# Attention and two mixture layers on one core: other planner durations and weights for ScalarE, a longer lag for the banks of h

## The chip, the cores and the metric

The kernel runs on one core of one Trainium2 chip. The time is device microseconds of one launch, the median of the runs shown. Engines are named PE (TensorE, matmuls; PEld is its weight load), DVE (VectorE), ACT (ScalarE), POOL (GpSimd) and SP (SyncE, which starts the DMAs). TensorE's granted clock is given as a share of full speed.

## The reference, cut to what matters

```python
def sm_attn(qq, kk, vv):                      # 8 batches, 8 heads of 64, 576 positions
    s = qq @ kk.transpose(0, 1, 3, 2) / 8
    a = np.exp(s - s.max(-1, keepdims=True))
    return (a / (a.sum(-1, keepdims=True) + 1e-9)) @ vv
p_packed = sm_attn(p, k, v)                   # 32 packed queries
x = sm_attn(q, p_packed, p_packed)            # -> 4608 tokens x 512
h = x @ w_in                                  # 512 -> 2048
g = h * np.tanh(np.log1p(np.exp(h)))
x2 = g @ w_out                                # 2048 -> 512
# experts: top one of 8 by x2 @ w_gate, weighted by its softmax probability
out = prob * (np.maximum(x2 @ w1[e], 0) @ w2[e])
```

## The kernel before

A batch has two halves of 288 tokens, 16 halves in all. Every float32 product is made of three matmuls on rounded parts (high times high, high times low, low times high). The attention's second step is folded into the first mixture's weights: `w_in` times the packed keys (`fold`, L457, eight matmuls of each of two PSUM tiles) gives `wp`, and the softmax of the scores (L510 and the DVE and ACT steps behind it, L517 to L553) is multiplied with it.

From about 66 us to 800 us the first mixture runs. Its pieces are, for each half and each 128 columns of h:

- the *product* (L595): six matmuls of 128 x 288 into a bank of `h`, a ring of two PSUM banks,
- `tanh` on ACT (L612), then the copy `hs` of the same bank (by the helper `copy_ways`, L244 on ACT or L245 on DVE). The copy's end frees the bank,
- after eight products, a *group*: the table of ACT is changed (L629), Arctan (L635) and Sin (L637) for four pairs of products, then on DVE the multiplication with hs (L640); `g1`, the rounded copy, by `copy_ways` on POOL, DVE or ACT; `g2`, the remainder, on DVE (L256),
- the *back* product (L608): three matmuls for each of four banks of `acc`.

At the next group's first tanh ACT loads the tanh table again (L612 ACT_TABLE_LOAD). In every batch PE also has the packed scores (L288), transposes (L313, L314), values (L321), and a transpose (L334) of the packed result `pd`; these share the ring `o` of two PSUM banks. Their softmax runs on DVE (maximum L298, L299) and ACT (exponential L302, with a table of its own). `at` and `ae` are the copies of the transposed softmax, `pk` the copy of the packed keys that the fold needs. Up to about 150 us the engines beside PE also convert the words of `w_in` and `w_out` (L398 to L434, `a`, `sgn`, `wi`, `woh`, `wol`).

From about 760 us on the experts run: L874 (h_p), ACT's relu L881, DVE's remainder L886, L894 (y), DVE's L900, with 8 pieces of an expert's weights loaded, rounded (`exh`, `copy_ways`) and subtracted (`exl`, `tensor_ways`) for every expert.

Nothing of this order is written by hand. Every piece is a step of a `Plan` (lines 34 to 165), which emits all steps in the order of a simulated clock in ns: it knows each step's cost on each engine that can do it, a `LATENCY` for each engine, rings with their buffers, and due times. Three things of it are touched here. `SLACK` is added to the end of the step that frees a ring's buffer before the buffer counts as free. `end` (line 106) estimates for a step with several engines when each would finish it; the cost there is multiplied by the engine's `WEIGHT`, and the engine with the earliest estimate takes it. The costs of steps on ACT stand at the calls, and for PSUM copies in `copy_ways`: 51 + 0.833 n on ACT, 69 + 1.03 n on DVE. The weights, costs and lag shape the order only; on the chip each engine takes its instructions in that order and waits for what they need.

Of the kernel before, what the change touches and what calls it, by code (L numbers as in the profile page):

```python
# [15 lines left out]
AF = mybir.ActivationFunctionType  # L16
# [26 lines left out]
             ls=1, x2=8, gm=2, os=2)  # L43


class Plan:
# [5 lines left out]
    LATENCY = dict(PE=70, DVE=128, ACT=190, Pool=117, SP=0, host=0)  # L52
    DMA_LATENCY, DMA_ISSUE, DMA_RATE, DMA_AHEAD = 1900, 450, 360.0, 937
    DMA_SLACK = 1000
    SLACK = dict(h=600)
    SLOWED = dict(DVE=0.3, Pool=0.5)
    WINDOW = 3413
    WEIGHT = dict(DVE=2.41, ACT=1.34, Pool=1.31)

    def __init__(self, rings):  # L60
        self.rings, self.steps = rings, []
# [12 lines left out]
    def run(self):  # L74
# [24 lines left out]
        for _ in range(len(self.steps)):  # L99
# [5 lines left out]

            def end(s, at, e):
                ahead = floor.get(e, now) + sum(cost for key, cost in alone.get(e, ()) if key < s["key"])
                return max(at, ahead) + s["ways"][e][0] * self.WEIGHT[e] + self.LATENCY[e]

            for e in able:  # L110
                mine = None
# [54 lines left out]
def packed_attention_moe_kernel(ctx, tc, pT, kT, v_main, v_tail, qT, w_in, w_out, wg, w1, w2, out):  # L166
# [66 lines left out]
    def step(engine, cost, emit, **kw):  # L233
        return plan.step([(engine, cost, emit)], **kw)

    def copy_ways(dst, src, n, psum=False):

        def on(run):
            def emit():
                d = dst()  # L240
                run(d, src())
            return emit

        ways = [("ACT", (51 if psum else 93) + 0.833 * n, on(lambda d, x: S.activation(out=d, in_=x, func=AF.Copy))),  # L244
                ("DVE", 69 + (1.03 if psum else 0.52) * n, on(lambda d, x: V.tensor_copy(out=d, in_=x)))]  # L245
        if not psum:
            ways.append(("Pool", 160 + 0.835 * n, on(lambda d, x: G.tensor_scalar(  # L247
                out=d, in0=x, scalar1=1.0, scalar2=1.0, op0=ALU.mult, op1=ALU.mult))))
        return ways
# [324 lines left out]
    def moe1(gr, due):  # L574
# [36 lines left out]
        def tanh(n, k):  # L611
            S.activation(out=part(n, "z", k), in_=tiles[n]["p", k], func=AF.Tanh, scale=0.5)  # L612

        for n in pairs:
            c = n % 16 // 4
            z1[n], hc[n] = [], []
            for k in range(2):
                at_k = due + (n + k - n0) * TI
                ins.append(step("PE", 798, lambda n=n, k=k: product(n, k),
                                  after=wp_done[b, c] + a2_done[i, g] + ins[-1:],  # L620
                                  takes=[("h", n + k)], frees=[("wa", ("w", b, c))] * (hf == 1 and (n + k) % 4 == 3)
                                  + [("hl", (i, g * parts))] * ((n + k) % 16 == 15 or parts and (n + k) % 8 == 7), due=at_k))
                z1[n].append(step("ACT", 291, lambda n=n, k=k: tanh(n, k), after=[ins[-1], *z1[n]] + sins.get(gr - 1, []),
                                  takes=[("z", n)] * (k == 0), due=at_k))
                hc[n].append(plan.step(copy_ways(lambda n=n, k=k: part(n, "hs", k), lambda n=n, k=k: tiles[n]["p", k], TK, True),
                                       after=[z1[n][k], *hc[n]], takes=[("hs", n)] * (k == 0), frees=[("h", n + k)], due=at_k))
                b_steps.extend([z1[n][k], hc[n][k]])
# [40 lines left out]
        def evac(d, engine):  # L668
            if d == 0 and not more:
                x2_load(i)  # L670
            if engine == "ACT":
                S.activation(out=x2f[i][:, d], in_=accs[i, d], func=AF.Copy)
            elif more:
                V.tensor_tensor(out=x2f[i][:, d], in0=x2f[i][:, d], in1=accs[i, d], op=ALU.add)
            else:
                V.tensor_copy(out=x2f[i][:, d], in_=accs[i, d])

        for d in range(4):
            ev.append(plan.step([(e, cost, lambda d=d, e=e: evac(d, e)) for e, cost in (("ACT", 291), ("DVE", 365))[more:]],
                                after=[outs[n + 1, d]] + ev[:1], takes=[("x2f", key)] * (d == 0 and not more),  # L680
                                frees=[("acc", (i, d, g * parts))], due=due))
        x2_done[key] = ev
# [43 lines left out]
    def gate_copy(i):  # L726
        l_s = tile_of("ls", [128, TK])
        S.activation(out=l_s, in_=gst[i], func=AF.Copy)
        gst[i] = l_s
# [78 lines left out]
    def gate(i, key, ld, due, exp_after=(), exp_before=None):  # L808
        b, hf = halves[i]
        mm = step("PE", 850, lambda: gate_mm(i), after=[ld, wg_done], takes=[("o", ("l", i))], frees=[("x2f", key)], due=due,  # L810
                  share=0.8)
        cp = step("ACT", 291, lambda: gate_copy(i), after=[mm], takes=[("ls", i)], frees=[("o", ("l", i))], due=due)
        tu = step("PE", 400, lambda: gate_turn(i), after=[cp], takes=[("o", ("t", i))], frees=[("ls", i)], due=due)
        mx = step("DVE", 600, lambda: gate_max(i), after=[tu], frees=[("o", ("t", i))], due=due)
        ex = step("ACT", 113, lambda: gate_exp(i), after=[mx, *exp_after], due=due)
# [63 lines left out]
    def moe2_hi(xk, f, early=False):  # L879
        h = tile_of("g", [128, 2, 2, TK], F32R)[:, :, 0] if early else tile_of("g2", [128, 2, TK], F32R)  # L880
        S.activation(out=h[:, 0], in_=hc[xk, f], func=AF.Relu)  # L881
        hc[xk, f] = hc[xk, f], h
# [25 lines left out]
    def moe2(n, due):  # L908
# [7 lines left out]
                       frees=[("wa", ("e", b, c, x)) for x in "hl"] * (hf == 1 and o == 3)  # L916
                       + x2_at(ring, ("x2", i)) * (f == 7), due=due)
        g = ("g" if early else "g2", ("y", n))
        hi = step("ACT", 291, lambda: moe2_hi(i, f, early), after=[y_in[n], last_g1 if early else open_c], takes=[g], due=due)
        lo = step("DVE", 369, lambda: moe2_lo(i, f), after=[hi], frees=[("h", ("y", n))], due=due)  # L920
        last, ahead[n] = i == NH - 1 and f > 5, (lo, g)
        for d, m in [(d, m) for d in range(4) for m in ((n - 1, n) if last else (n,))] * (not last or f == 7):
# [212 lines left out]
```

## Time and profile before

| | |
|---|---|
| median of 3 runs | 1211.97 us (1211.04 to 1212.27) |
| profiled execution | 1210.29 us |
| its span | 1208.5 us |
| mean granted clock | 0.993 |
| PE busy | 1161.8 us (96%) |
| DVE busy | 676.0 us (56%) |
| ACT busy | 651.1 us (54%) |
| POOL busy | 224.5 us (19%) |

The span is the time between the first and the last record of the profiled execution. An engine's busy time leaves out register, branch, semaphore and DMA-issuing instructions. A wait is the idle time of an engine ahead of an instruction, with the instruction that ended it: "PE h L595 <- ACT hs L244" is PE idle ahead of a matmul of line 595 into h until ACT's copy of line 244.

### The profile page before, as it was taken

What the parts mean: (1) busy time and instruction counts of PE and PEld (TensorE: products, weight loads), DVE (VectorE), ACT (ScalarE), POOL (GpSimd) and SP (SyncE); (2) the same over time, 40 slices, a digit from 0 to 9 for tenths busy, and PEclk for the clock granted to TensorE, in tenths of its full rate; (3) what the DMA queues carried; (4) which work ended last, traced back from release to release, by engine and by line L of the source; (5) the groups of instructions that cost most, each with busy time, mean ns of one, the idle gap of its engine ahead of it and who ended that gap; (6) DMA issues with size and microseconds to landing.
All of it is one profiled execution on the core that took longest, in us unless ns stands there. A gap on an engine that the chain in (4) does not pass through costs nothing.

```text
span 1208.5 us, 23614 instructions
## 1 busy us (share of the span) xinstructions
PE 1161.8 (96%) x9680; PEld 1075.2 (89%) x9681; DVE 676.0 (56%) x1237; ACT 651.1 (54%) x1335; POOL 224.5 (19%) x214
## 2 busy tenths in 40 slices
PE   4699999999999999999999999999999999999998
PEld 1478898898898898898898899999999999999998
DVE  4999955564455454454454464466556473737442
ACT  3687787777777777777777778212122121212110
POOL 2344411011011021021021022112213030302110
PEclk9889999999999999999999999999999999999999
DMA  8856533421331321321321141133425151524411
GB/s 294 307 193 223 206 138 125 175 110 56 153 129 56 134 110 56 133 110 56 133 110 56 55 145 55 50 130 139 152 77 189 58 189 62 189 86 143 146 45 41
DMA packets 37642, 151.48 MB, mean 125 GB/s; under 512 B 4888, under 2 KB 5528, under 8 KB 33944
## 3 DMA queue, kind: packets, MB, share of 16 engines
q1 hardware_dynamic: 37528, 149.90, 34.1%
q8 instruction: 78, 1.28, 0.4%
q14 instruction: 36, 0.29, 0.1%
HBM read 122.04 MB, written 27.84 MB: 124 GB/s over the span
## 4 chain that ended last, share of the span: by engine, by line
PE 76%; DVE 10%; ACT 8%; issue 2%; DMA 2%; POOL 1%; SPq 0%; DVEq 0%; ACTq 0%; POOLq 0%
PE x2p L608 25%; PE y L894 15%; PE h_p L874 15%; PE h L595 14%; PE w_ps L457 2%; DVE z L640 2%; DVE g L256 1%; ACT L612 1%; DMA eraw<-w 1%; ACT z L635 1%; PE o L321 1%; ACT L629 1%; ACT z L612 1%; PE o L510 1%; ACT hs L244 1%
## 5 line engine op out<-in xcount | busy, mean ns | idle before, releaser
L608 PE MATMUL x2p<-g,woh 128*128 128x288 f32 x2048 | 416.6, 297 | 0.0
L608 PEld LDWEIGHTS x2p<-g,woh 128*128 128x128 f32 x2048 | 327.4, 188 | 14.4 <-issue 13.6
L608 PE MATMUL x2p<-g,wol 128*128 128x288 f32 x1024 | 301.9, 295 | 0.0
L595 PEld LDWEIGHTS h<-hl,wp 128*128 128x128 f32 x1536 | 215.2, 191 | 47.0 <-ACT hs L244 35.6
L595 PE MATMUL h<-hl,wp 128*128 128x288 f32 x1536 | 242.1, 303 | 12.6 <-ACT hs L244 12.6
L894 PE MATMUL y<-g,exh 128*128 128x288 f32 x1024 | 211.2, 298 | 1.2 <-DVE os L900 0.5
L881 ACT ACTIVATE g<-h_p 128x288 fp32r<-128x288 f32 x128 | 52.4, 410 | 279.7 <-PE h_p L874 257.4
L608 PEld LDWEIGHTS x2p<-g,wol 128*128 128x128 f32 x1024 | 192.2, 188 | 0.0
L640 DVE TENSOR_TENSOR z<-z,hs 128x576 f32<-128x576 f32 x128 | 95.3, 780 | 147.1 <-ACT z L637 147.1
L894 PEld LDWEIGHTS y<-g,exh 128*128 128x128 f32 x1024 | 162.6, 188 | 9.0 <-issue 4.3
L612 ACT ACTIVATE z<-h 128x288 f32<-128x288 f32 x256 | 105.7, 413 | 108.9 <-PE h L595 102.9
L247 POOL TENSOR_SCALAR g<-z 128x576 fp32r<-128x576 f32 x85 | 78.7, 927 | 454.0 <-DVE z L640 364.9
L874 PE MATMUL h_p<-x2h,exh 128*128 128x288 f32 x512 | 152.0, 297 | 0.0
L874 PE MATMUL h_p<-x2l,exh 128*128 128x288 f32 x512 | 151.0, 295 | 0.0
L874 PE MATMUL h_p<-x2h,exl 128*128 128x288 f32 x512 | 150.7, 294 | 0.0
L894 PE MATMUL y<-g,exl 128*128 128x288 f32 x512 | 150.4, 294 | 0.0
L886 DVE SCALAR_TENSOR_TENSOR g<-h_p,g 128x288 fp32r<-128x288 f32 x128 | 57.7, 451 | 138.4 <-ACT g L881 138.4
L244 ACT ACTIVATE hs<-h 128x288 f32<-128x288 f32 x256 | 104.7, 411 | 0.9 <-DVE z L640 0.9
L256 DVE TENSOR_TENSOR g<-z,g 128x576 fp32r<-128x576 f32 x128 | 94.6, 762 | 15.3 <-POOL g L247 15.2
L874 PEld LDWEIGHTS h_p<-x2h,exh 128*128 128x128 f32 x512 | 96.0, 187 | 0.9 <-DVE x2h L702 0.5
L894 PEld LDWEIGHTS y<-g,exl 128*128 128x128 f32 x512 | 96.5, 189 | 0.0
L874 PEld LDWEIGHTS h_p<-x2l,exh 128*128 128x128 f32 x512 | 96.5, 188 | 0.0
(127 smaller groups left out, 1334.5 us busy)
## 6 DMA issues: line engine op xcount, KB each, us to landing
eraw<-w SPq DMA_DIRECT2D x64, 512.0 KB, 6.2
wi<-wi_d SPq DMA_DIRECT2D x24, 1024.0 KB, 6.7
x2f<-x_d SPq DMA_DIRECT2D x22, 576.0 KB, 4.3
x_d<-x2f SPq DMA_DIRECT2D x20, 576.0 KB, 2.8
raw<-kT SPq DMA_DIRECT2D x16, 576.0 KB, 7.5
q<-qT SPq DMA_DIRECT2D x16, 576.0 KB, 5.3
out<-os SPq DMA_DIRECT2D x15, 576.0 KB
raw<-v_main SPq DMA_DIRECT2D x16, 512.0 KB, 8.5
```

Source lines behind the costliest of these rows:

```text
L244: ways = [("ACT", (51 if psum else 93) + 0.833 * n, on(lambda d, x: S.activation(out=d, in_=x, func=AF.Copy))), ("DVE", 69 + (1.03 if psum ...
L247: ways.append(("Pool", 160 + 0.835 * n, on(lambda d, x: G.tensor_scalar(out=d, in0=x, scalar1=1.0, scalar2=1.0, op0=ALU.mult, op1=ALU.mult))))
L256: engine.tensor_tensor(out=d, in0=a(), in1=b(), op=op)
L457: T.matmul(out=t[i][quarter(x)], lhsT=pk[own[i], b, x], rhs=w_i[c][own[i], x], start=True, stop=True)
L595: T.matmul(out=h, lhsT=wp_t[b, c][:, xw, kt, 128 * o:128 * o + 128], rhs=a2[i, g][:, xa, kt], start=(m == 0), stop=(m == 5))
L608: T.matmul(out=accs[i, d], lhsT=w_o[c][xw][:, o, 128 * d:128 * d + 128], rhs=tiles[n]["g"][:, xg, k], start=(m == 0 and (f == 0 or f == 8 ...
L612: S.activation(out=part(n, "z", k), in_=tiles[n]["p", k], func=AF.Tanh, scale=0.5)
L640: g0 = step("DVE", 669, lambda n=n, z=z: V.tensor_tensor(out=z(), in0=z(), in1=tiles[n]["hs"], op=ALU.mult), after=[si, *hc[n]], frees=[(" ...
L874: T.matmul(out=h_p, lhsT=ex_t[ek, c][xw][:, k, 128 * o:128 * o + 128], rhs=x2s[xk][xx][:, k], start=(n == 0), stop=(n == 11))
L881: S.activation(out=h[:, 0], in_=hc[xk, f], func=AF.Relu)
L886: V.scalar_tensor_tensor(out=h[:, 1], in0=h_p, scalar=0.0, in1=r32(h[:, 0]), op0=ALU.max, op1=ALU.subtract)
L894: T.matmul(out=accs[xk, d], lhsT=ex_t[ek, 2 + c][xw][:, o, 128 * d:128 * d + 128], rhs=hc[xk, f][:, xh], start=(f == 0 and n == 0), stop=( ...
```

## The change

`SLACK` of h goes from 600 to 1000 ns. `WEIGHT` becomes a pair: the first as before, the second when the planner's clock is past `EARLY`, 150 us. In the second DVE's factor is 1.3 (2.41 before), ACT's 1.9 (1.34 before), POOL's the same. Single reads of PSUM by ACT get a cost 16 ns higher: 67 instead of 51 in `copy_ways`, 307 instead of 291 for the tanh, the copy of the result x2f, the gate's copy and the experts' relu. Lines behind line 55 move on by two, so L595 is L597 in the changed kernel, L244 and L245 are L246 and L247, L302 is L304.

```diff
-    SLACK = dict(h=600)
+    SLACK = dict(h=1000)
     SLOWED = dict(DVE=0.3, Pool=0.5)
     WINDOW = 3413
-    WEIGHT = dict(DVE=2.41, ACT=1.34, Pool=1.31)
+
+    EARLY = 150000
+    WEIGHT = dict(DVE=2.41, ACT=1.34, Pool=1.31), dict(DVE=1.3, ACT=1.9, Pool=1.31)
...
-                return max(at, ahead) + s["ways"][e][0] * self.WEIGHT[e] + self.LATENCY[e]
+                return max(at, ahead) + s["ways"][e][0] * self.WEIGHT[now > self.EARLY][e] + self.LATENCY[e]
...
-        ways = [("ACT", (51 if psum else 93) + 0.833 * n, on(lambda d, x: S.activation(out=d, in_=x, func=AF.Copy))),
+        ways = [("ACT", (67 if psum else 93) + 0.833 * n, on(lambda d, x: S.activation(out=d, in_=x, func=AF.Copy))),
...
-                z1[n].append(step("ACT", 291, lambda n=n, k=k: tanh(n, k), after=[ins[-1], *z1[n]] + sins.get(gr - 1, []),
+                z1[n].append(step("ACT", 307, lambda n=n, k=k: tanh(n, k), after=[ins[-1], *z1[n]] + sins.get(gr - 1, []),
...
-        hi = step("ACT", 291, lambda: moe2_hi(i, f, early), after=[y_in[n], last_g1 if early else open_c], takes=[g], due=due)
+        hi = step("ACT", 307, lambda: moe2_hi(i, f, early), after=[y_in[n], last_g1 if early else open_c], takes=[g], due=due)
```

How many instructions of a kind each engine has, counted over the whole order:

| copies | before | after |
|---|---|---|
| hs, h out of its bank | ACT 256 | ACT 128, DVE 128 |
| wp, rounded | ACT 64 | ACT 39, DVE 25 |
| at | ACT 16 | ACT 5, DVE 11 |
| ae | DVE 16 | DVE 5, ACT 11 |
| g1 | ACT 15, DVE 28, POOL 85 | ACT 5, DVE 40, POOL 83 |
| exh | ACT 22, DVE 7, POOL 35 | DVE 16, POOL 48 |
| exl | DVE 57, POOL 7 | DVE 64 |
| x2l (a part of x2) | DVE 16, POOL 16 | DVE 32 |

On PE, nearly every stretch between two pairs of products holds 12 matmuls of the back product where 9 stood, for the same work in all. At a group that follows the packed transposes (L334), in a middle batch, PE's order also turns round. L595 (L597) is the product, L510 (L512) the scores, L457 (L459) the fold, L608 (L610) the back product. Before:

```order
L608 MATMUL x2p_5264<-g,woh 128x288 x2
L608 MATMUL x2p_5264<-g,wol 128x288
L595 MATMUL h<-hl,wp 128x288 x6
L510 MATMUL o<-q,pk 32x288 x8
L595 MATMUL h<-hl,wp 128x288 x12
L457 MATMUL w_ps<-wi,pk 32x512 x8
L595 MATMUL h<-hl,wp 128x288 x12
```

After:

```order
L610 MATMUL x2p_5243<-g,wol 128x288
L512 MATMUL o<-q,pk 32x288 x8
L597 MATMUL h<-hl,wp 128x288 x12
L610 MATMUL x2p_5774<-g,woh 128x288 x2
L610 MATMUL x2p_5774<-g,wol 128x288
L459 MATMUL w_ps<-wi,pk 32x512 x8
L597 MATMUL h<-hl,wp 128x288 x12
```

The scores now stand ahead of the group's first product instead of behind it, and three matmuls of a back product stand ahead of the fold.

On DVE, in the same batch, where the packed softmax's maximum (`sm`) stands among the steps of a group. L640 (L642) is the multiplication with hs, L245 (L247) a copy, L256 (L258) the remainder. Before:

```order
L640 TENSOR_TENSOR z_5291<-z_5291,hs_5293 128x576
L640 TENSOR_TENSOR z_5320<-z_5320,hs_5322 128x576
L256 TENSOR_TENSOR g_5425<-z_5291,g_5425 128x576
L298 TENSOR_REDUCE sm_5442<-ex_5387 128x1
L299 TENSOR_SCALAR sm_5442<-sm_5442 128x1
L298 TENSOR_REDUCE sm_5457<-ex_5399 128x1
L299 TENSOR_SCALAR sm_5457<-sm_5457 128x1
L307 TENSOR_SCALAR sm_5442<-sm_5442 128x1
L308 RECIPROCAL sm_5442<-sm_5442 128x1
L256 TENSOR_TENSOR g_5455<-z_5320,g_5455 128x576
```

After:

```order
L642 TENSOR_TENSOR z_5297<-z_5297,hs_5299 128x576
L300 TENSOR_REDUCE sm_5432<-ex_5378 128x1
L301 TENSOR_SCALAR sm_5432<-sm_5432 128x1
L300 TENSOR_REDUCE sm_5447<-ex_5395 128x1
L301 TENSOR_SCALAR sm_5447<-sm_5447 128x1
L258 TENSOR_TENSOR g_5438<-z_5297,g_5438 128x576
L309 TENSOR_SCALAR sm_5432<-sm_5432 128x1
L310 RECIPROCAL sm_5432<-sm_5432 128x1
L309 TENSOR_SCALAR sm_5447<-sm_5447 128x1
L310 RECIPROCAL sm_5447<-sm_5447 128x1
L642 TENSOR_TENSOR z_5329<-z_5329,hs_5331 128x576
```

Both maxima now come ahead of the third pair's remainder and of the fourth pair's multiplication. Behind that pair's rounding copy and remainder, this queue goes on with copies of h for the next group.

On ACT, at the end of the prelude (about 62 to 66 us before). L329 (L331) is `pd`, the packed result; L612 (L614) the tanh. Before:

```order
L329 ACTIVATE pd_684<-o_712,sm_597 128x64
L637 ACTIVATE z_566<-z_566,b_pi_171 128x576
L637 ACTIVATE z_604<-z_604,b_pi_171 128x576
L244 ACTIVATE pk_168<-o_740 128x128
L612 ACT_TABLE_LOAD
L612 ACTIVATE z_750<-h_638 128x288
L244 ACTIVATE hs_765<-h_638 128x288
```

After:

```order
L246 ACTIVATE g_697<-z_449 128x576
L246 ACTIVATE at_705<-o_690 128x512
L639 ACTIVATE z_562<-z_562,b_pi_171 128x576
L637 ACTIVATE z_608<-z_608,b_half_169 128x576
L639 ACTIVATE z_608<-z_608,b_pi_171 128x576
L331 ACTIVATE pd_684<-o_710,sm_594 128x64
L614 ACT_TABLE_LOAD
L614 ACTIVATE z_743<-h_636 128x288
L246 ACTIVATE hs_747<-h_636 128x288
L614 ACTIVATE z_743<-h_648 128x288
L246 ACTIVATE hs_747<-h_648 128x288
L246 ACTIVATE pk_168<-o_751 128x128
```

The table load and two pairs of tanh and copy now stand ahead of `pk`, and a rounding copy of g ahead of `at`.

## Rows read from the trace of the kernel before

**Rows 1.** Busy time by stretch: each engine's us (count), then clock, DMA share.

```profile
62.00:66.00 4.00, 2.53 (x18) 0.50 (x18) 3.97 (x6) 3.97 (x9) 2.80 (x3) 0.50 0.86 279
66.00:150.00 84.00, 79.56 (x624) 71.22 (x625) 79.94 (x111) 67.00 (x138) 39.33 (x41) 0.98 0.57 201
150.00:800.00 650.00, 641.21 (x5608) 591.97 (x5607) 329.08 (x566) 469.69 (x956) 91.26 (x96) 1.00 0.27 102
800.00:1209.00 409.00, 401.92 (x3066) 391.27 (x3064) 218.95 (x463) 77.61 (x165) 74.76 (x47) 1.00 0.34 119
```

**Rows 2.** PE's waits from 66, 150 and 800 us: total, times, longest.

```profile
PE h L595 <- ACT hs L244: 3.8, 3, 1.6
...
PE h L595 <- ACT hs L244: 8.8, 17, 1.1
...
PE y L894 <- DVE os L900: 0.5, 2, 0.2
PE y L894 <- ACT g L881: 0.5, 1, 0.5
```

**Rows 3.** Chain of waits, one run of back products: start, us.

```profile
690.18 9.54 PE x2p L608 x72
```

**Rows 4.** Timeline at a group's start: start us, us, engine, instruction, [idle before].

```profile
499.50 0.29 PE L608 MATMUL x2p<-g,wol 128*128 128x288 f32 x1
...
500.07 1.87 PE L595 MATMUL h<-hl,wp 128*128 128x288 f32 x12 [0.27 <-ACT hs L244]
```

**Rows 5.** Timeline at the packed softmax's exponential.

```profile
538.49 0.76 DVE L256 TENSOR_TENSOR g<-z,g 128x576 fp32r<-128x576 f32 x1 [0.57 <-POOL g L247]
...
539.16 0.74 DVE L298 TENSOR_REDUCE sm<-ex 128x1 f32<-128x576 f32 x1
...
540.17 1.28 ACT L302 ACT_TABLE_LOAD   x1 [2.45 <-DVE sm L299]
...
542.39 0.29 PE L608 MATMUL x2p<-g,wol 128*128 128x288 f32 x1
...
543.29 0.40 ACT L244 ACTIVATE hs<-h 128x288 f32<-128x288 f32 x1
...
543.74 0.66 PE L595 MATMUL h<-hl,wp 128*128 128x288 f32 x3 [1.06 <-ACT hs L244]
```

**Rows 6.** Timeline at two groups that begin around the scores.

```profile
293.34 0.93 PE L595 MATMUL h<-hl,wp 128*128 128x288 f32 x5 [0.69 <-ACT hs L244]
...
564.05 1.28 ACT L612 ACT_TABLE_LOAD   x1 [0.42 <-PE h L595]
...
566.11 0.92 PE L595 MATMUL h<-hl,wp 128*128 128x288 f32 x5 [0.51 <-ACT hs L244]
...
567.10 1.09 PE L457 MATMUL w_ps<-wi,pk 64*32 64x512 f32 x16
```

**Rows 7.** Timeline at the longest wait between 66 and 150 us.

```profile
139.87 0.66 ACT L400 ACTIVATE a<-word 128x512 f32<-128x512 f32 x1
...
140.87 0.80 PE L595 MATMUL h<-hl,wp 128*128 128x288 f32 x4 [1.62 <-ACT hs L244]
```

**Rows 8.** The page's groups: reads of 288 columns from PSUM, mean ns.

```profile
L886 DVE SCALAR_TENSOR_TENSOR g<-h_p,g 128x288 fp32r<-128x288 f32 x128 | 57.7, 451 | 138.4 <-ACT g L881 138.4
L244 ACT ACTIVATE hs<-h 128x288 f32<-128x288 f32 x256 | 104.7, 411 | 0.9 <-DVE z L640 0.9
```

**Rows 9.** Timeline at the end of the prelude.

```profile
63.58 0.26 ACT L244 ACTIVATE pk<-o 128x128 f32<-128x128 f32 x1
...
63.89 1.96 PE L457 MATMUL w_ps<-wi,pk 64*32 64x512 f32 x16 [1.02 <-ACT pk L244]
```

**Rows 10.** Timeline at the load of an expert's weights.

```profile
925.31 0.41 ACT L881 ACTIVATE g<-h_p 128x288 fp32r<-128x288 f32 x1 [2.78 <-PE h_p L874]
...
928.95 0.45 DVE L886 SCALAR_TENSOR_TENSOR g<-h_p,g 128x288 fp32r<-128x288 f32 x1
929.60 2.74 DVE L245 CAST exh<-eraw 128x1024 fp32r<-128x1024 f32 x1 [0.20 <-DMA eraw<-w]
```

More of the change, by code (lines that the diff above doesn't have):

```diff
@@ L678, in moe1 @@
         for d in range(4):
-            ev.append(plan.step([(e, cost, lambda d=d, e=e: evac(d, e)) for e, cost in (("ACT", 291), ("DVE", 365))[more:]],
+            ev.append(plan.step([(e, cost, lambda d=d, e=e: evac(d, e)) for e, cost in (("ACT", 307), ("DVE", 365))[more:]],
                                 after=[outs[n + 1, d]] + ev[:1], takes=[("x2f", key)] * (d == 0 and not more),
@@ L811, in gate @@
                   share=0.8)
-        cp = step("ACT", 291, lambda: gate_copy(i), after=[mm], takes=[("ls", i)], frees=[("o", ("l", i))], due=due)
+        cp = step("ACT", 307, lambda: gate_copy(i), after=[mm], takes=[("ls", i)], frees=[("o", ("l", i))], due=due)
         tu = step("PE", 400, lambda: gate_turn(i), after=[cp], takes=[("o", ("t", i))], frees=[("ls", i)], due=due)
```

## The prediction

> **What bounds the kernel now.** I read the busy time by stretch first [rows 1]. From 66 us on TensorE (PE) is busy 80 of 84, 641 of 650 and 402 of 409 us: the change takes no matmul away, so all it can give back is idle time of PE, and all the harm it can do is new idle time. The waits come next [rows 2]. Up to 800 us nearly everything that PE waits for is a bank of `h`: the copy of h out of PSUM (`hs`, on ScalarE, ACT) is the last reader of a bank, and there are two banks. That is 3.8 us in 3 waits from 66 to 150 us, and 8.8 us in 17 waits up to 800 us. The experts' stage, behind that, has no such copy, and waits of 1.0 us in all. So the gain is bounded by 12.6 us and by what each restart costs beside its wait. At a group's start the last back product's matmul (L608) begins at 499.50 and the product (L595) at 500.07 [rows 4]; the pace is 0.133 us for a matmul, 9.54 us for 72 [rows 3], so the loss is 0.57 - 0.13 = 0.44 us, where the wait says 0.27. With 0.16 more for each of 20 waits the bound is 12.6 + 3.2 = **15.8 us**.
>
> The waits from 150 us on have three forms.
> *Exponential*, four times 1.06 [rows 5]: VectorE (DVE) takes the softmax's maximum only from 539.16, behind a subtraction (L256) that had itself waited 0.57 us for GpSimd (POOL). ACT loads the table from 540.17, and with two exponentials and a tanh in between, the copy that frees the bank starts at 543.29. PE began its last back product's matmul before that at 542.39.
> *Scores*, three times 0.51 and once 0.69 [rows 6]: the tanh table is loaded at a group's first product (564.05), and PE has only eight score matmuls and one more product to do until the first bank is back.
> *Group start*, seven waits of about 0.3 [rows 4]: table load, tanh and copy against two products and nine matmuls of the back product. Two waits that are left are under 0.15.
>
> **The change part by part.** No work is added or removed. What moves is the engine of a copy, how long the planner keeps PE from a bank, and the place of some matmuls.
>
> 1. *The longer lag (SLACK of h from 600 to 1000 ns) and ACT's durations, 16 ns longer.* A bank comes free later in the plan, so the plan puts more back products between two pairs of products: 12 matmuls in the order where 9 stood, in nearly every pair. Three more are 3 x 0.133 = 0.40 us of cover for each wait. By themselves they cost nothing: the longer runs of back products that follow have three or six less.
>
> Group starts: loss 0.44, cover 0.40, so 7 x 0.40 = **-2.8** (bounds 0 and -3.1).
> Scores: the order has the eight score matmuls first, then two products in one piece, three back matmuls and a fold of 1.09 us [rows 6], then the next bank. The first product ends 0.8 us into the piece; table load 1.28, tanh and copy 0.41 each [rows 6, 8] free its bank at 2.9, or 3.0 with what lies between instructions; PE has 1.6 + 0.4 + 1.1 = 3.1 us of work until then. The wait goes: 3 x (0.51 + 0.16) + 0.69 + 0.16 = 2.9, of which I take **-2.7**. If only the three back matmuls count, it is 4 x 0.40 = -1.6.
>
> 2. *The exponential.* The order of DVE now puts both maxima ahead of the subtraction that had waited, and ahead of the last multiplication. That takes 0.57 us of waiting and two instructions of about 0.76 [rows 5] out of the way: the table load comes up to 2.1 us sooner, at 538.1. From table load to copy were 543.29 - 540.17 = 3.1 us; the same three instructions stand there now (two exponentials, then tanh), so the bank is free at about 538.1 + 3.1 + 0.4 + 0.1 = 541.7. PE, with its three more back matmuls, asks for it at 542.5 + 0.4 = 542.9. What hides the maxima is the work of POOL and ACT ahead of them: if the third multiplication is late, the table is late with it, one for one. For that I leave 0.45 of each loss of 1.06 + 0.16 = 1.22 standing: 4 x 0.77 = **-3.1** (bounds 0 and -4.9).
>
> 3. *66 to 150 us.* The weights don't change there (EARLY is 150 us), only lag and durations do. In the longest wait, 1.62, the copy was late because a conversion (`a`, 0.66) stood ahead of it on ACT [rows 7]. Loss in this stretch: 3.8 + 3 x 0.16 = 4.3. The order has 12 or 15 back matmuls where 6 or 9 stood. I take two thirds, **-2.8** (bounds 0 and -4.3): DVE is busy 80 of 84 us there [rows 1], so a wait can move rather than end.
>
> 4. *Weights after 150 us.* DVE is cheap in the plan now and ACT dear; half of the copies of h, 128 of 256, go to DVE. One costs 0.41 on ACT and 0.45 on DVE, by its nearest row, another read of 288 columns from PSUM [rows 8]. That is 0.04 us more until the bank is back, but ACT can begin the next bank's tanh 0.3 us sooner, so I cost it at nothing; its cover is the 12 back matmuls. Queued behind it on DVE are the multiplications and subtractions that feed the back product; DVE was busy 329 of 650 us [rows 1] and gets 128 x 0.45 = 58 us more. The packed softmax's copies out of PSUM (`at`) go to DVE too and share the two banks of `o`: a new wait in each of six batches, between 0 and 0.5 us (a wait of rows 6), of which I take 0.2: **+1.2** (bounds 0 and +3).
>
> The Trainium skill speaks against this part: VectorE: DVE Perf Modes, section Specifications, has VectorE closer to SBUF and ScalarE closer to PSUM. The rows agree, 0.45 against 0.41 [rows 8]; if PE waited for the difference at each of the 128 copies, it would be 128 x 0.04 = 5 us, and the sum -2.5 in place of -7.5.
>
> 5. *The prelude, up to 66 us.* Here too the order differs through lag and durations. Before, ACT copied `pk` at 63.58, ahead of its tanh table; PE's fold started at 63.89 after a wait of 1.02 [rows 9]. In the new order ACT has a rounding copy of g ahead of `at` (576 columns; from 0.26 us for 128 and 0.41 for 288 I estimate 0.7) and one more `pd`, less one conversion that leaves: some 0.5 to 1.2 us. And the table load and two tanh with two copies stand ahead of `pk`: 1.28 + 4 x 0.3 = 2.5. The fold comes up to 3.7 us later; nine back matmuls are done meanwhile, 1.2 us at pace. Net **+2.5** (bounds 0, if something else holds the fold anyway, and +3.7). The granted clock is 0.50 in this stretch [rows 1], the lower of the two levels; more idle time may keep it there longer, which the range takes in.
>
> 6. *Experts.* ACT gives up its 22 rounding copies of weights; DVE takes nine and POOL 13 of them, and DVE takes POOL's seven subtractions. PE's order is nearly the same. DVE's L886 started 3.2 us after the end of the ACT step it follows (925.72 to 928.95) and PE didn't wait [rows 2, 10]. So **0**, between -1 (all waits of that stage) and the price of the slower rival.
>
> Sum: -2.8 - 2.7 - 3.1 - 2.8 + 1.2 + 2.5 = -7.7, of which I keep **-7.5**. The profiled execution, 1210.29, goes to 1202.8; the median of the runs shown, 1.7 us above it, goes from 1211.97 to **1204.5**.
>
> **The rivals.**
> *All of the waits go.* All 15.8 are covered, the prelude and the `o` banks still cost: -15.8 + 2.5 + 1.2 = -12.1, so 1200. For it: 12 back matmuls in every pair, and half of the copies off ACT. Against it: table load, tanh and copy are as long as before.
> *The gain is swallowed.* The plan's order isn't the chip's time: the exponential's chain stays late (nothing of 3.1), the early waits move (nothing of 2.8), the prelude loses 3.7: -7.7 + 3.1 + 2.8 + 1.2 = -0.6, so 1211.4; with two of the three 1208.5 to 1210.2. For it: tanh stands behind both exponentials now. This is also the case in which the change doesn't do what it says.
> *Slower: DVE is late for the experts.* It has 16 rounding copies where seven stood, two in each load of an expert. At 2.74 us [rows 10] the nine are 25 us more of DVE, in front of L886; a delay of L886 beyond the 3.2 us is on PE's path. With half of the 25 there it is 1204.5 + 12.5 = 1217. It decides when two such copies stand between an L881 and its L886. Against it: seven of them ran with waits of 1.0 us in all [rows 2], and POOL's subtraction, which ran beside one, is gone.
>
> By the Trainium skill (SBUF — State Buffer, Who interferes with whom) a DVE copy in a two-port mode and a GpSimd instruction lock each other out of a shared port pair for a whole instruction. If each of the nine casts met a rounding copy on POOL so, the time would be this rival's 1217. No row here shows PE waiting for it.
>
> **How the numbers follow.** Forecast 0.55 (1202 to 1208), all of the waits 0.14 (1198 to 1202), swallowed 0.18 (1208.5 to 1212.5), slower 0.13 (from 1214.5). The range takes the first, part of the second and the third: 1199.5 to 1212.5. A measurement of this kernel can tell about 0.2%, 2.4 us, from no change. Faster by more: 0.55 + 0.14 + a little of the third, 0.71; within it: 0.16; slower by more: 0.13.
>
> **What the changed profile would show.** Waits of L595 for hs from 150 to 800 us under 3 us, in place of 8.8; the exponential's table load about 2 us sooner against the products beside it; the fold in the prelude at about 66 to 67.5; PE busy as before from 800 us on. I am wrong if PE waits for DVE's copy of h in many groups, if the clock stays at 0.50 beyond 70 us, or if L894 waits for L886 at the loads of experts.

## The result and the profile after

The changed kernel takes 1200.13 us in the median of four runs (1199.23 to 1201.89), the kernel before 1211.51 beside it: a ratio of 0.9912, with a 95% interval from 0.9897 to 0.9928. The time lies in the range of the prediction, 4.4 us below its 1204.5. The profiled execution took 1200.09 us with a span of 1198.3, which is 10.2 us less than before (1210.29 and 1208.5).

Busy time of the changed kernel by stretch, in the columns of [rows 1]:

```profile
62.00:66.00 4.00, 3.19 (x18) 2.34 (x15) 2.83 (x5) 3.94 (x8) 2.60 (x4) 0.50 0.58 170
66.00:150.00 84.00, 80.28 (x637) 69.56 (x638) 78.79 (x111) 62.77 (x130) 40.86 (x45) 0.96 0.60 209
150.00:800.00 650.00, 648.85 (x5682) 602.41 (x5681) 432.88 (x814) 399.64 (x758) 81.81 (x84) 1.00 0.28 104
800.00:1198.00 398.00, 390.81 (x2986) 381.63 (x2984) 218.72 (x463) 55.36 (x140) 62.89 (x42) 1.00 0.33 119
```

From 150 to 800 us PE is now busy 648.9 of 650 us, where it was 641.2. DVE has 104 us more to do there and ACT 70 less. PE's waits of the changed kernel from 66, 150 and 800 us, to be set beside [rows 2]:

```profile
PE h L597 <- ACT hs L246: 1.6, 3, 0.8
PE w_ps L459 <- ACT pk L246: 0.9, 1, 0.9
PE x2p L610 <- ACT x2f L674: 0.9, 1, 0.9
PE x2p L610 <- DVE g L258: 0.7, 1, 0.7
...
PE h L597 <- ACT hs L246: 0.9, 4, 0.2
PE x2p L610 <- DVE g L258: 0.2, 1, 0.2
...
PE h_p L876 <- DVE g L888: 1.8, 3, 0.8
```

The 17 waits of the middle stretch, 8.8 us, are four of 0.9 us. They are the four exponentials; the group starts and the scores have none left. From 66 to 150 us the waits for h fell from 3.8 to 1.6 us, but two of 0.9 and 0.7 us for the back product's banks (x2p) came, and one of 0.9 at the fold.

*Exponential.* Timeline of the changed kernel at the place of [rows 5]:

```profile
532.38 0.75 DVE L642 TENSOR_TENSOR z<-z,hs 128x576 f32<-128x576 f32 x1
533.04 0.74 DVE L300 TENSOR_REDUCE sm<-ex 128x1 f32<-128x576 f32 x1
...
534.05 1.28 ACT L304 ACT_TABLE_LOAD   x1 [0.96 <-DVE sm L301]
534.05 1.76 PE L597 MATMUL h<-hl,wp 128*128 128x288 f32 x12
...
537.10 0.29 PE L610 MATMUL x2p<-g,wol 128*128 128x288 f32 x1
537.17 0.39 ACT L246 ACTIVATE hs<-h 128x288 f32<-128x288 f32 x1
...
537.62 1.06 PE L597 MATMUL h<-hl,wp 128*128 128x288 f32 x6 [0.23 <-ACT hs L246]
```

The table load begins with the products beside it, no longer 0.8 us behind them, and its copy starts 3.12 us later, as it did (543.29 - 540.17). Of the wait of 1.06 us, 0.23 is left. The 0.83 between them is the table load's alone, since PE has 12 back matmuls between these two pairs of products in both kernels. Matmuls into x2p (busy, count, clock) before and after:

```profile
539.60:543.60 4.00, 1.74 (x12) 1.00 0.00 0
534.30:537.50 3.20, 1.74 (x12) 1.00 0.00 0
```

*Scores.* Timeline at the place of [rows 6]:

```profile
556.31 1.28 ACT L614 ACT_TABLE_LOAD   x1
...
557.62 1.85 PE L597 MATMUL h<-hl,wp 128*128 128x288 f32 x12
...
558.71 0.41 ACT L614 ACTIVATE z<-h 128x288 f32<-128x288 f32 x1 [1.11 <-PE h L597]
559.34 0.42 DVE L247 COPY hs<-h 128x288 f32<-128x288 f32 x1
...
559.80 1.09 PE L459 MATMUL w_ps<-wi,pk 64*32 64x512 f32 x16
```

ACT has loaded the table 1.3 us ahead of the group's first product and then waits for PE. Before, it came to the load with four copies of x2f behind it, and only when the product was done.

*Group start.* Timeline at the place of [rows 4]:

```profile
493.10 1.28 ACT L614 ACT_TABLE_LOAD   x1 [0.39 <-PE h L597]
...
494.70 0.41 ACT L246 ACTIVATE hs<-h 128x288 f32<-128x288 f32 x1
...
495.11 0.29 PE L610 MATMUL x2p<-g,wol 128*128 128x288 f32 x1
495.24 1.79 PE L597 MATMUL h<-hl,wp 128*128 128x288 f32 x12
```

The last back matmul and the product stand 0.13 us apart, PE's pace. The copy's end at 495.11 falls together with the end of the twelve matmuls: three more of them were just enough.

*Prelude.* Timeline of the changed kernel at the place of [rows 9]:

```profile
63.60 1.28 ACT L614 ACT_TABLE_LOAD   x1
...
66.08 0.31 ACT L246 ACTIVATE pk<-o 128x128 f32<-128x128 f32 x1
...
66.44 1.96 PE L459 MATMUL w_ps<-wi,pk 64*32 64x512 f32 x16 [0.88 <-ACT pk L246]
```

The fold comes 2.55 us later than before (63.89), behind table load, two tanh and two copies.

### The profile page after: what moved, and what is told of

The parts are those of the page before. It is cut to its first block, busy times and chain, and to the rows that moved or that the text cites. A ratio compares the mean times of both kernels' runs of the same rounds, so it can differ in the third digit from the quotient of the medians.

```text
span 1198.3 us, 23588 instructions
## 1 busy us (share of the span) xinstructions
PE 1158.8 (97%) x9680; PEld 1075.2 (90%) x9681; DVE 775.6 (65%) x1481; ACT 554.7 (46%) x1107; POOL 204.9 (17%) x198
## 4 chain that ended last, share of the span: by engine, by line
PE 82%; DVE 8%; issue 3%; ACT 3%; DMA 2%; POOL 1%; SPq 0%; POOLq 0%; ACTq 0%; DVEq 0%
PE x2p L610 29%; PE y L896 15%; PE h_p L876 15%; PE h L597 15%; PE w_ps L459 2%; DVE z L642 1%; DVE exl L258 1%; DVE g L258 1%; DMA eraw<-w 1%; PE o L323 1%; PE o L512 1%; PE l_p L725 1%; POOL sgn L414 1%; PE o L290 1%; PE lt_p L737 1%
## 5 line engine op out<-in xcount | busy, mean ns | idle before, releaser
L610 PE MATMUL x2p<-g,woh 128*128 128x288 f32 x2048 | 420.0, 298 | 2.0 <-DVE g L258 1.0
L610 PEld LDWEIGHTS x2p<-g,woh 128*128 128x128 f32 x2048 | 328.5, 188 | 24.6 <-issue 20.7
L610 PE MATMUL x2p<-g,wol 128*128 128x288 f32 x1024 | 302.3, 295 | 0.0
L597 PE MATMUL h<-hl,wp 128*128 128x288 f32 x1536 | 240.9, 302 | 3.3 <-ACT hs L246 3.3
L597 PEld LDWEIGHTS h<-hl,wp 128*128 128x128 f32 x1536 | 214.8, 190 | 27.9 <-issue 14.5
L610 PEld LDWEIGHTS x2p<-g,wol 128*128 128x128 f32 x1024 | 192.8, 188 | 0.0
L614 ACT ACTIVATE z<-h 128x288 f32<-128x288 f32 x256 | 105.0, 411 | 162.0 <-PE h L597 144.2
L876 PE MATMUL h_p<-x2h,exh 128*128 128x288 f32 x512 | 151.9, 297 | 1.8 <-DVE g L888 1.8
L876 PE MATMUL h_p<-x2l,exh 128*128 128x288 f32 x512 | 151.0, 295 | 0.0
L876 PE MATMUL h_p<-x2h,exl 128*128 128x288 f32 x512 | 150.8, 295 | 0.0
L888 DVE SCALAR_TENSOR_TENSOR g<-h_p,g 128x288 fp32r<-128x288 f32 x128 | 58.0, 453 | 123.6 <-ACT g L883 123.0
L249 POOL TENSOR_SCALAR exh<-eraw 128x1024 fp32r<-128x1024 f32 x48 | 71.3, 1498 | 342.2 <-DMA eraw<-w 329.5
L642 DVE TENSOR_TENSOR z<-z,hs 128x576 f32<-128x576 f32 x128 | 93.6, 764 | 52.2 <-ACT z L639 52.2
L247 DVE COPY hs<-h 128x288 f32<-128x288 f32 x128 | 58.4, 456 | 89.0 <-ACT z L614 89.0
L258 DVE TENSOR_TENSOR exl<-eraw,exh 128x1024 fp32r<-128x1024 f32 x64 | 98.2, 1548 | 9.5 <-POOL exh L249 9.5
L258 DVE TENSOR_TENSOR g<-z,g 128x576 fp32r<-128x576 f32 x128 | 96.5, 774 | 9.1 <-POOL g L249 8.8
L876 PEld LDWEIGHTS h_p<-x2h,exh 128*128 128x128 f32 x512 | 96.0, 187 | 2.8 <-DVE g L888 2.8
```

The lines of the kernel that those rows point to most:

```text
L258: engine.tensor_tensor(out=d, in0=a(), in1=b(), op=op)
L597: T.matmul(out=h, lhsT=wp_t[b, c][:, xw, kt, 128 * o:128 * o + 128], rhs=a2[i, g][:, xa, kt], start=(m == 0), stop=(m == 5))
L610: T.matmul(out=accs[i, d], lhsT=w_o[c][xw][:, o, 128 * d:128 * d + 128], rhs=tiles[n]["g"][:, xg, k], start=(m == 0 and (f == 0 or f == 8 ...
L642: g0 = step("DVE", 669, lambda n=n, z=z: V.tensor_tensor(out=z(), in0=z(), in1=tiles[n]["hs"], op=ALU.mult), after=[si, *hc[n]], frees=[(" ...
L876: T.matmul(out=h_p, lhsT=ex_t[ek, c][xw][:, k, 128 * o:128 * o + 128], rhs=x2s[xk][xx][:, k], start=(n == 0), stop=(n == 11))
L888: V.scalar_tensor_tensor(out=h[:, 1], in0=h_p, scalar=0.0, in1=r32(h[:, 0]), op0=ALU.max, op1=ALU.subtract)
```

## Experiments

Theory A says that the cover did it: the lag puts twelve back matmuls between two pairs of products. Theory B says that the engines did it: ACT was late since it had too many copies, and the weights take them off it. Each variant is timed in three rounds against the kernel before; the changed kernel's time is that of the result. The last three columns are of each kernel's profiled execution: PE's waits for hs, the end of the last back product, and the rest of the span behind it, which is the experts' stage. Ahead of that end the order has 12 matmuls of L874; where it has 24 or none, 1.6 us (12 matmuls) are taken from one of the two and given to the other.

| kernel | median, us | ratio (interval) | waits for hs, 150 to 750 us | last back product ends | rest, us |
|---|---|---|---|---|---|
| before | 1211.3 | 1 | 8.8 | 772.4 | 436.1 |
| changed | 1200.13 | 0.9912 (0.9897 to 0.9928) | 0.9 | 762.4 | 435.9 |
| lag alone | 1202.23 | 0.9928 (0.9912 to 0.9945) | 0.9 | 763.9 | 436.8 |
| weights alone | 1203.72 | 0.9937 (0.9915 to 0.9959) | 1.6 | 763.3 | 441.4 |
| ACT's durations alone | 1211.59 | 1.0005 (0.9995 to 1.0014) | 6.8 | 773.3 | 434.9 |
| lag and weights | 1202.13 | 0.9929 (0.9913 to 0.9946) | 0.9 | 764.5 | 436.6 |
| lag and durations | 1204.71 | 0.9941 (0.9925 to 0.9958) | 1.3 | 762.9 | 441.5 |
| changed, hs on ACT | 1201.0 | 0.9910 (0.9894 to 0.9927) | 0.9 | 761.6 | 438.4 |

**The three parts, each alone.**

```diff
-    SLACK = dict(h=600)
+    SLACK = dict(h=1000)
```

> The kernel before with the lag of h at 1000 ns alone: weights and ACT's durations as before, so 254 of 256 copies of h stay on ACT, and 12 back matmuls stand between pairs of products. Theory A (cover: the three more back matmuls end the waits): from 150 to 800 us the loss of 11.5 us falls by about 7 (group starts 2.8, exponentials 1.6, scores 2.7), early part 2.3 better, prelude as before: about 1202. Theory B (engines: ACT comes late since it does too many copies): the exponentials and scores keep their waits, only the group starts' 0.4 each go: about 1207.

The lag alone gives 9.1 of the 11.4 us, with 254 copies of h still on ACT. PE's waits of this kernel from 150 to 750 us, and behind that:

```profile
PE h L595 <- ACT hs L244: 0.9, 4, 0.2
...
PE y L894 <- DVE os L900: 0.7, 2, 0.4
PE h_p L874 <- DVE g L886: 0.3, 1, 0.3
```

The waits are those of the changed kernel, and the time is theory A's number, but that it fits is luck. From the fold at 205 us to the end of the back product this execution gains 10.0 us, where A had about 7. At 205 us it stands 1.6 us behind the kernel before (207.0 and 205.4), where A had it 2.3 ahead, and the rest is 0.7 longer. Nor is the lag only cover: at the exponential there are 15 back matmuls where 12 stood (0.40 us), and the maxima stand ahead of DVE's subtraction here too, so that the table load begins 0.39 us behind the products and not 0.82.

```diff
-    WEIGHT = dict(DVE=2.41, ACT=1.34, Pool=1.31)
+    EARLY = 150000
+    WEIGHT = dict(DVE=2.41, ACT=1.34, Pool=1.31), dict(DVE=1.3, ACT=1.9, Pool=1.31)
...
-                ... * self.WEIGHT[e] + self.LATENCY[e]
+                ... * self.WEIGHT[now > self.EARLY][e] + self.LATENCY[e]
```

> The kernel before with the pair of weights alone: lag 600 and ACT's durations as before, so nine back matmuls stay between pairs, and 108 copies of h and most copies of at and some of wp and x2f go to DVE behind 150 us. Up to 150 us nothing changes. Theory A: the waits at group starts stay (0.3 each), the exponentials gain 3, scores little: about 1208. Theory B: scores and exponentials lose their waits as in the changed kernel, group starts too since ACT reaches its table load earlier: about 1204.

The weights alone take the same waits away, with nine back matmuls between pairs. PE's waits of this kernel from 150 to 750 us, and behind that:

```profile
PE h L597 <- ACT hs L246: 1.6, 8, 0.3
...
PE h_p L876 <- DVE g L888: 4.4, 5, 1.8
PE y L896 <- ACT ls L730: 0.5, 1, 0.5
```

So theory B has its number too, with runs from 1201.3 to 1206.6. At the exponential the table load begins 2.3 us ahead of the products here (533.39 and 535.65), so nine back matmuls are enough. The two parts remove the same waits, and their gains (9.1 and 7.6 by the medians) don't add. The weights alone lose in the experts' stage, where PE waits 4.4 us for DVE and the rest is 5.3 us longer in this execution, the slowest of its four. About 1.7 of that is the clock's (below, on the clock).

```diff
-        ways = [("ACT", (51 if psum else 93) + 0.833 * n, ...
+        ways = [("ACT", (67 if psum else 93) + 0.833 * n, ...
...
-  step("ACT", 291, ...        # tanh, x2f, gate copy, relu
+  step("ACT", 307, ...
```

> The kernel before with ACT's durations 16 ns longer alone. Its prelude is the changed kernel's (products 12, fold, products 12; pk behind the tanh table and two copies). If the durations alone set the prelude, the fold there starts at about 66.4 instead of 63.9 us and the waits from 150 us on stay: about 1213.5, between 1211 and 1215. If the prelude's loss came from the lag, the time is that of before, 1211.5.

ACT's durations alone change nothing that can be measured: the fold of the prelude starts at 67.5 us, 3.6 later than before, and most of it comes back in small pieces (waits for hs 6.8 instead of 8.8, a rest 1.2 us shorter).

> The change without ACT's longer durations. The prelude's order is that of before (18 products ahead of the second fold). If ACT's durations cost the prelude 2.5 us and bring nothing from 150 us on, the time is 1197.6, 2.5 below the changed kernel's 1200.1; if the 16 ns matter for the spacing later, it is 1200 or more.

This one missed: with the order of before in the prelude (fold at 64.4 us) it isn't faster than the changed kernel but 2 us slower, with intervals that overlap. What the prelude keeps is lost between 66 and 150 us, in waits of 2.7 us for DVE's low half of wp and of 1.2 for the same in the scores, which the changed kernel doesn't have, and in the clock, which fell at the end of the longer of them. The wait, and PE's time (busy, count, clock) around it:

```profile
116.12 2.55 PE L459 MATMUL w_ps<-wi,pk 64*32 64x512 f32 x16 [2.67 <-DVE wp L462]
...
115.00:123.00 8.00, 6.88 (x36) 0.57 0.80 241
```

and the changed kernel:

```profile
115.00:123.00 8.00, 7.22 (x60) 1.00 0.62 220
```

The lag alone has the same wait and a fall of the clock behind it; the profiles of the seven kernels with lag and ACT's durations in the prelude have neither. So the durations, which change nothing by themselves, go with a better order up to 150 us once the lag is there.

**Does a copy of h have to leave ACT?** The changed kernel, with all 256 copies of h on ACT.

```diff
-   hc[n].append(plan.step(copy_ways(..., TK, True),
+   hc[n].append(plan.step(copy_ways(..., TK, True)[:1],
```

> The changed kernel, but the copies of h may only be done by ACT (all 256); everything else of the change stays: lag, durations and the pair of weights for the other steps. Theory A (cover of 12 back matmuls is enough): 1200, waits of products from 150 to 800 us about 1 us as in the changed kernel. Theory B (half of the copies must leave ACT): ACT is 58 us busier, the exponentials' and scores' waits come back in part, 2 to 5 us: 1202 to 1205.

No: 1201.0, and the waits for hs are 0.9 us as in the changed kernel. The half of the copies on DVE, the largest move of the change, isn't what the gain rests on.

**Lag and durations, without the weights.**

> The changed kernel without the pair of weights: lag 1000 and ACT's longer durations, the old weights throughout. The order up to 150 us is the changed kernel's. If the weights bring nothing once the lag is there, it is 1200.1 less the 1.8 us that L876 waits for DVE's L888 in the experts' stage, so 1198.5 to 1199.5. If the weights carry a part of the gain from 150 to 800 us, it is 1202 or more.

It missed on the side of the weights, at 1204.71. The profiled execution, the slowest of its four, is 6.1 us behind the changed kernel's, and 5.6 of that lie in the rest (441.5 against 435.9), where PE waits 3.6 us for DVE's L886 and 1.1 for L900. Ahead of it the weights are worth little. That put the experts' stage in question, in which the change had seemed to do nothing.

**The experts' stage.** The first attempt gave the old weights back from 740 us on, the second also the old lag and durations up to 66 us.

```diff
-    EARLY = 150000
+    EARLY, LATE = 150000, 740000
...
-                ... self.WEIGHT[now > self.EARLY][e] + ...
+                ... self.WEIGHT[self.EARLY < now < self.LATE][e] + ...
```

> The changed kernel, but the first pair of weights comes back at 740 us, ahead of the experts' stage: the order is the changed kernel's up to there, and the expert's rounding copies go back to ACT. If DVE's share of them causes the waits of L876 for L888 (1.8 us, three times), they go: 1198.3. If not, 1200.

> As the last one, but lag and ACT's durations are those of before up to 66 us, so the prelude's order is the order of before, with its fold at 63.9 us in place of 66.4. If the prelude's 2.5 us are a plain loss, the time is 2.5 below the last one, about 1196; if they are given back between 66 and 150 us (the back matmuls done early are then missing as cover), it is the same as the last one, 1198 to 1199.

Both missed: 1203.06 (ratio 0.9937, 0.9913 to 0.9960) and 1204.47 (0.9936, 0.9912 to 0.9960). They end the first mixture earlier than the changed kernel (760.5 and 761.4 against 762.4 us) and lose in the rest, 440.2 and 445.3 us against 435.9. So the old pair doesn't help there. That the second pair is the better one for the experts isn't shown, though: the intervals overlap with the changed kernel's. The second attempt's profile is the slowest of its four (1208.89, where two of the others took 1202), with the clock at its lower level behind a wait of 2.7 us. And the table has good and bad rests with either pair: 434.9 to 441.5 us with the first, 435.9 to 441.4 with the second. Nor is the prelude settled: in the second attempt the fold that stood 1.6 us earlier in the prelude stands 0.6 earlier at 205 us, which is less than executions of one order differ by there (below, on the clock).

What the pairs of weights do to the experts' pieces is in DVE's group rows (count, busy, mean ns), here of the kernel before:

```profile
L256 DVE TENSOR_TENSOR exl<-eraw,exh 128x1024 fp32r<-128x1024 f32 x55 | 74.3, 1378 | 24.3 <-POOL exh L247 15.8 <-issue 8.5
L245 DVE CAST exh<-eraw 128x1024 fp32r<-128x1024 f32 x7 | 18.6, 2658 | 0.2 <-DMA eraw<-w 0.2
```

and of the changed kernel:

```profile
L258 DVE TENSOR_TENSOR exl<-eraw,exh 128x1024 fp32r<-128x1024 f32 x59 | 90.7, 1548 | 9.5 <-POOL exh L249 9.5
L247 DVE CAST exh<-eraw 128x1024 fp32r<-128x1024 f32 x14 | 12.2, 872 | 14.5 <-DMA eraw<-w 14.5
```

The rounding copy took 2658 ns in the kernel before, where each of the seven ran beside one of POOL's subtractions (2.6 us each); without these it takes 872. Of all 16 in the changed kernel, eleven ran with nothing on POOL beside them and took 0.68 to 0.70 us, the other five, beside POOL's rounding copies, 0.68 to 1.56. DVE's subtraction became slower, 1378 to 1548, beside POOL's 43 rounding copies. And L888 can be queued behind both. A wait of the changed kernel, by the timelines of PE and DVE:

```profile
974.68 1.53 DVE L247 CAST exh<-eraw 128x1024 fp32r<-128x1024 f32 x1
976.13 1.21 DVE L258 TENSOR_TENSOR exl<-eraw,exh 128x1024 fp32r<-128x1024 f32 x1
977.26 0.45 DVE L888 SCALAR_TENSOR_TENSOR g<-h_p,g 128x288 fp32r<-128x288 f32 x1
...
977.76 0.40 PE L876 MATMUL h_p<-x2h,exh 128*128 128x288 f32 x1 [0.79 <-DVE g L888]
```

Three kernels ask which of it counts. The kernel before, with the subtractions on DVE alone:

```diff
-   ... ALU.subtract, 1024, b > 0),
+   ... ALU.subtract, 1024, False),
```

> The kernel before, with the experts' subtraction (exl) on DVE alone: POOL loses its seven, and the plan gives the rounding copies (exh) to ACT and POOL, none to DVE. All up to the experts' stage is before's. If the old weights' experts' stage isn't hurt by POOL's subtractions, it is as before: 1211.3, waits of L874 and L894 there of 1 us. If DVE's rounding copies cost anything in it, 1 us less at most: 1210.

1209.75, ratio 0.9986 (0.9976 to 0.9995): 1.5 us by the medians, at the edge of what can be told; the rest is 435.6 us in place of 436.1, with one wait of 2.0 for L886. Then the changed kernel with all rounding copies behind the first expert's on ACT, and the changed kernel with these steps later in the plan:

```diff
-   hi = plan.step(copy_ways(..., 1024),
+   hi = plan.step(copy_ways(..., 1024)[:3 - 2 * (b > 0)],
```

> The changed kernel with the experts' rounding copies (exh, all but those of the first expert) on ACT alone, which is busy 55 of 398 us in that stage; neither DVE nor POOL has one. If L876 waits for L888 because rounding copies stand ahead of it on DVE or POOL slows DVE's subtractions, the waits (1.8 us) go, and DVE's subtractions take 1.2 us throughout: 1198.3. If L888 is late because it is queued behind a subtraction whose weights come late by DMA, they stay: 1200.

```diff
-   ... takes=[(ring, ("e", b, p, x)) for x in "hl"] * (part == 0), due=due)
+   ... takes=[(ring, ("e", b, p, x)) for x in "hl"] * (part == 0), due=due, lag=1500 * (b > 0))
```

> The changed kernel, with 1500 ns more in the plan between an expert's load and its rounding copy (not the first expert). DVE's and POOL's rounding and subtractions then stand later in their queues against L888. If L888 is late because it stands behind a subtraction whose weights come late by DMA, the waits of L876 go: 1198.3. If DVE simply has too much in a row, they stay or grow (the plan gives DVE 37 rounding copies): 1200 to 1203.

With the rounding copies on ACT it takes **1195.69** us (1194.93 to 1196.56; ratio 0.9869, 0.9853 to 0.9886): faster than both kernels. The list of PE's waits behind 750 us is empty, the rest is 433.3 us, and DVE's subtraction is back at its length without POOL:

```profile
L258 DVE TENSOR_TENSOR exl<-eraw,exh 128x1024 fp32r<-128x1024 f32 x59 | 71.7, 1223 | 20.4 <-ACT exh L246 19.7
```

The later place in the plan takes the waits for L888 away too, at 1197.56 (0.9885, 0.9868 to 0.9901), with the rest at 433.9 and 35 rounding copies on DVE. So a rounding copy on DVE doesn't by itself make L888 late. What does isn't separated: both kernels change the order in front of L888, and both take rounding copies from POOL (48 in the changed kernel, 6 and 27 in these), beside which DVE's subtraction is slower. Of the 4.5 us by which the best kernel's span is shorter than the changed one's, 2.6 lie in the rest; the others lie ahead of it, in the same order of instructions (below, on the clock). The medians are 4.4 us apart and the runs don't overlap; how much of that is the clock's, one profile of each doesn't show.

Last, the same without the pair of weights: lag and durations, subtractions on DVE, rounding copies on ACT.

> The change without its pair of weights (254 copies of h on ACT), and in the experts' stage the rounding copies on ACT alone and the subtractions on DVE alone. Its relatives took 1204.7 (without the pair, experts' pieces as the old weights share them) and 1195.7 (with the pair, rounding copies on ACT). If the pair of weights matters only through who does the experts' pieces, this is 1195.7 too, with no wait of L874 for L886. If the pair also carries a part of the gain ahead of 740 us, it is 1198 or more.

1199.79 (0.9899, 0.9877 to 0.9920): 4.9 us better than lag and durations alone (1204.71), and 4.1 short of the best, or 3.6 by the ratios. In the experts' stage, at 435.3 us, L874 still waits 1.4 us for L886; what is left of the weights' work there is x2l and the order of the pieces, and which of these counts isn't shown. Ahead of it, 0.8 us behind the best one at the eighth fold (127.2 and 126.3 us), with the same order to there, it is 2.2 behind at the end of the back product: 1.4 us that the weights carry from 150 us on. Of these, 0.6 are waits of 0.4 for a copy of h on DVE and 0.2 at a gate; the others aren't assigned.

## Why the prediction was right, and where it wasn't

**What bounds the kernel** was read rightly: banks of h, with 15.8 us as the bound. 150 to 800 us gave 7.9 us of visible waiting for h back, with 13 restarts of 0.16 less that is 10.0; from the fold at 205 us to the end of the back product the changed kernel gained 10.1. The median, 1200.13, isn't where the forecast was put (1202 to 1208) but in the band of the rival by which all of the waits go (1198 to 1202, a chance of 0.14). From 150 us on that rival came true. Ahead of it it didn't, and it counted 1.2 for the banks of o, which cost nothing; so its number is in part luck as well.

**Group starts** (-2.8): right, all seven are gone, 3.1. **Scores** (-2.7): all gone, 2.9. The step's chain was wrong, though: it let the table load begin at the first product's end. In the changed kernel ACT, relieved by the weights, has it loaded before the product starts. The lag alone does as well, as the first experiment shows. **Exponential** (-3.1): right, 0.39 of each loss of 1.22 stays (0.23 and the 0.16 of a restart), where 0.45 was left, so 3.3. Its middle was not, and the number came right by luck. The table load is 0.8 us sooner against the products beside it (0.82 us behind their start before, level with it now), not 2.1, since the third multiplication itself stood late in DVE's queue. The three more back matmuls, 0.40 us in the prediction, aren't there at all: 12 stood at this place already, and 12 stand there now. With 0.8 in place of 2.1 and no cover, the loss that the step left standing, 0.45 for such a case, was about what stayed.

**Banks of o** (+1.2): the step that failed outright. From 150 us on PE has no wait for them in the changed kernel, nor in the others with these weights. The bound of 0.51 was taken from a wait for a bank of h, which has another chain.

**66 to 150 us and the prelude** (-2.8 and +2.5): their sum, -0.3, is near what came, 0.1 (the fold at 205 us starts at 205.4 before, 205.5 after), but both terms were too large. The fold in the prelude is 2.55 us later, where up to 3.7 was worked out; less the 1.2 of the nine back matmuls done meanwhile, the net loss is 1.4 and not 2.5. From there to 205 us, 1.2 come back and not 2.8. The early waits moved in part, as the prediction feared: those for h fell from 3.8 to 1.6 us, and 1.6 us for the banks of x2p came. The clock, which stood only in the range's upper bound, took another part: it stayed at the lower level longer (0.58 from 68 to 73 us, 0.93 before). Other executions of the changed order stood at 203.5 to 204.9 us there.

**Experts** (0, and the slower rival): the time is the same, 436.1 and 435.9 us. The rival's place was right, L876 waiting for L888, and so was its kind; its price was wrong. It took the 2.74 us of a rounding copy from a row in which POOL's subtraction ran beside it, while the change took these subtractions off POOL: the copies cost 0.87. By the Trainium skill (SBUF — State Buffer, Who interferes with whom) an instruction of DVE with two inputs in SBUF also contends with a GpSimd instruction that reads SBUF; the 1548 ns of the subtraction beside POOL's rounding copies, and 1223 without them, agree.

**The sum.** The profiled executions differ by 10.2 us, the sum said 7.7, of which 7.5 were kept. Of the 2.5 between, 1.2 are the banks of o, 0.7 the waits that ended more fully (3.1 + 2.9 + 3.3 against 8.6), -0.4 the first 205 us, and 1.0 aren't assigned. What is left to the 11.4 us of the medians is the scatter of single executions.

**Part 4 at nothing** was right for the copies of h (1201.0 with all of them on ACT), and the forecast's split was wrong only in this: parts 1 and 4 each end most of the waits alone, and part 6 can hold a loss of several us (the rest was 433.3 to 445.3 us over all kernels, a part of it by the clock), which the even sum of the change hid.

## What to carry to other kernels

Two parts of a change that remove the same wait don't add; try each alone before crediting one. Where a price is taken from a row, look at what ran beside it, and whether the change leaves that neighbour there: a copy of 2.66 us was one of 0.87 when its neighbour left. A time that fits isn't enough either: take it apart by stage, since terms that are wrong can cancel. And when a stage comes out even, look for what was gained and lost inside it: the experts' stage, the same to 0.2 us, held the next 2.6 us.

## What the runs showed of the hardware

The order of the changed kernel and that of the best one are the same up to 740 us, but their clocks weren't. TensorE's time by stretch (busy, count, granted clock), the changed kernel:

```profile
66.00:68.00 2.00, 1.56 (x16) 0.50 0.94 293
68.00:73.00 5.00, 5.00 (x29) 0.58 0.83 292
```

the best one:

```profile
66.00:68.00 2.00, 1.73 (x21) 1.00 0.96 348
68.00:73.00 5.00, 5.00 (x46) 1.00 0.58 211
```

and the kernel before:

```profile
68.00:73.00 5.00, 5.00 (x41) 0.93 0.51 202
```

With the clock at its lower level of the two for most of 68 to 73 us, PE did 29 instructions where it did 46 at full clock, and the two executions are 2.0 us apart at 205 us (205.5 and 203.5), which stays to the end of the back product (762.4 and 760.5). That is a scatter of single executions of one order: kernels with equal orders up to there stood at 203.5, 204.1, 204.9 and 205.5 us. Differences of 1 to 2 us between single profiles up to there can't be read as an effect of a change, and the medians of the runs are to be taken. Behind it single profiles can be compared: from the fold at 205 us to the one at 677 us three executions of this order took 471.5, 471.6 and 471.5 us.

Behind 75 us the clock fell again, ahead of the kernel's end, in five of the profiled executions, each time within 2 us of the end of a long wait of PE. Two of them are in the experts' stage, weights alone and then the second attempt on the experts (the wait, then PE's busy time, count and clock):

```profile
982.09 0.40 PE L876 MATMUL h_p<-x2h,exh 128*128 128x288 f32 x1 [1.79 <-DVE g L888]
...
982.00:987.00 5.00, 4.91 (x25) 0.66 0.00 0
```

```profile
923.54 0.37 PE L881 MATMUL h_p<-x2h,exh 128*128 128x288 f32 x1 [2.65 <-DVE g L893]
...
923.00:928.00 5.00, 4.46 (x22) 0.66 0.07 26
```

A mean of 0.66 over 5 us is 3.4 us at the lower level, half of which, 1.7 us, is an estimate of what it cost. The other three are lag alone (a wait of 2.7 us at 113 us), durations alone (2.5 at 124) and lag and weights (2.7 at 113, above). It isn't the same for every wait: behind three of 1.9 to 2.0 us (lag and durations, the kernel before with DVE's subtractions, and the changed kernel with hs on ACT) the clock stayed up. That the wait brought the fall isn't shown by a run of its own.
